# One tile fewer turned on TensorE in every second block, and key quarters loaded behind the query loads

## The chip, the cores and the metric

The kernel runs on one core of a Trainium2 chip. The metric is the device time of one execution in microseconds (us); of several executions the median counts. TensorE (PE in the profile, PEld its weight loads), VectorE (DVE), ScalarE (ACT), GpSimd (POOL) and SyncE (SP), which here only issues DMAs, each run their own stream of instructions in order and wait for each other by semaphores.

## The reference

Attention against pooled keys, and a gated MLP on the highest-scoring rows of each batch. Float32 in and out.

```
kv_pool = kv.reshape(4, 96, 4, 8, 4, 128).mean(axis=(2, 4))       # 768 keys a batch
k = v = kv_pool.reshape(4, 768, 128) @ w_sr
a = softmax(q @ k^T / sqrt(128))                                  # 12288 queries a batch
x = a @ v
per batch: take the 128 rows of x with the highest x . w_gate
           x[row] += sigmoid(score) * (relu(x[row] @ w1) @ w2)
```

## The kernel before

The queries are cut into 192 blocks of 256, 48 a batch, and one loop runs over them (`i`). A block has 256 x 768 scores, seen as 12 tiles of 128 x 128: two halves of 128 queries (`j`), six key tiles each. Every score tile is computed from split operands with three products into one of two PSUM buffers `s` (`S_together`), each of three banks of 512 columns. Then, for block `i`:

- VectorE takes the row maximum over all 1536 columns (`s_max`, tile `m`), once in every block: its starts mark the blocks in the trace.
- ScalarE takes the exponentials in three pieces (`exp`), into `am` in SBUF.
- The weights `a` are needed with the keys on the partitions, so every tile has to be turned, and each is needed twice, as a float16 high half and a bfloat16 low half. There are three ways for a tile, and `turned(n)` and `own(n)` say how many tiles go which way. **Turned on TensorE**: `turn_pe` transposes the last `turned(n)` tiles back into the `s` bank; ScalarE casts them to the high half (`to_high(n, 2)`) and VectorE subtracts for the low half (`to_low(n, 2, dve)`), both straight into `at`. **Turned by DMA**: ScalarE casts `main(n)` columns of `am` to `hl` (`to_high(n, 0)`), GpSimd makes their low halves (`to_low(n, 0, pool)`), and one DMA transpose on SP's queue (`turn`) carries both halves from `hl` to `at`. **Own**: where `own(n)` is 256, two of the tiles that go by DMA keep their exponentials in the `s` bank; ScalarE casts them from there (`to_high(n, 1)`), and VectorE rather than GpSimd makes their low halves, one block later (`to_low(i - 1, 1, dve)`, right behind `s_max(i)`).
- The product with the values (`AV`, tile `o_two`) of block `n` runs five blocks later, in two halves of 18 matmuls. Then `sums`, `recip`, `gate_scores` and `finish` on VectorE scale the rows, and every second block a store of 256 KB is issued.

In the kernel before, `turned(n)` is 2 and `own(n)` is 0 in all 144 blocks of batches 0 to 2. In batch 3, `turned(n)` is 0 in even and 1 in odd blocks, and `own(n)` is 256 in both (the last three blocks are handled apart).

Beside the blocks, tasks are advanced at marked points of the loop: `next_keys` pools and projects the keys of the next batch (GpSimd adds, seven blocks for one of six key tiles of 1 MB), `topk` searches the threshold of the batch before in 32 steps, one a block, each with a small count matmul, and `pick` runs the MLP. Batch 3 has no next keys to make.

SP's queue takes in order: in block `i` the transpose of block `i - 1`; in odd blocks the load of the queries of two blocks (256 KB, eight blocks ahead); in even blocks a store. The key tiles come in quarters of 256 KB: before, `next_keys` issues them, in steps of two blocks within a key tile, in odd blocks for one tile and in even blocks for the next, and at four even blocks at the end of a batch (`early`). The buffer `kvp` holds three key tiles.

Of the kernel before, what the change touches and what calls it, by code (L numbers as in the profile page):

```python
# [20 lines left out]
B, N, C = 4, 12288, 128  # L21
HK, WK, R = 384, 32, 4
M = (HK // R) * (WK // R)
KT = M // P
# [44 lines left out]
def attention_topk_mlp(ctx, tc, a, outs, capacity):  # L69
# [56 lines left out]
    def load_kv(b, kc, parts=1, t=None):  # L126
        late = t is not None
        if not late:
            t = kvp.tile([P, 2, P // 2, TAPS], F32, name="kv_raw")
        n = 2 // abs(parts)  # L130
        for i in range(abs(parts)):
            if parts > 0 or late == (i > 0):
                sp.dma_start(out=t[:, i * n:(i + 1) * n], in_=a["kv"][:, b, kc, i * n:(i + 1) * n])
        return t

    def load_quarter(b, kc, k, t=None):
        if t is None:
            t = kvp.tile([P, 2, P // 2, TAPS], F32, name="kv_raw")
        i, lo = k // 2, k % 2 * P // 4
        sp.dma_start(out=t[:, i, lo:lo + P // 4], in_=a["kv"][:, b, kc, i, lo:lo + P // 4])  # L140
        return t
# [3 lines left out]
    def load_q(b, ch, lo=0, hi=CHUNK):  # L145
        if (b, ch) not in qraw:
            qraw[b, ch] = qp.tile([P, CHUNK], F32, name="q_raw")
        sp.dma_start(out=qraw[b, ch][:, lo:hi], in_=a["q"][:, b, ch, lo:hi])
# [163 lines left out]

    def next_keys(b):
        new_keys(b)
        raws = {}
        pend = []
        ready = None

        def after(kc):
            if kc % 2:  # L320
                pair = kc // 2
                soon.append(lambda: (v_max(b, pair), pair == KT // 2 - 1 and v_peak(b)))
                pend.extend([lambda: None, lambda: (split_k(b, 2 * pair, 2 * pair + 2, 0), split_k(b, 2 * pair, 2 * pair + 2, 1))])

        for kc in range(KT):
            if kc == 0:
                raws[0] = early.pop(b) if b in early else load_kv(b, 0)
            if kc + 1 < KT:
                raws[kc + 1] = load_quarter(b, kc + 1, 0)
            t = raws[kc]  # L330
            pooled = kvs.tile([P, P], F32, name="pooled")
            u = kvu.tile([P, P, TAPS // 2], F32, name="kv_sum")
            t = t.rearrange("p h k t -> p (h k) t")
            adds = [(u[:, 32 * h:32 * h + 32], t[:, 32 * h:32 * h + 32, 0:8], t[:, 32 * h:32 * h + 32, 8:16]) for h in range(4)]
            adds += [(u[:, :, 0:4], u[:, :, 0:4], u[:, :, 4:8]), (u[:, :, 0:2], u[:, :, 0:2], u[:, :, 2:4]),
                     (pooled, u[:, :, 0], u[:, :, 1])]
            for h, (o, x, y) in enumerate(adds):
                if ready and h == 1:
                    yield from key_tile(b, kc - 1, ready)
                    after(kc - 1)  # L340
                yield "e" if h == len(adds) - 1 else "d"
                pool.tensor_tensor(out=o, in0=x, in1=y, op=ALU.add)
                if h == len(adds) - 1:
                    yield "d"
                if h in (1, 3, 5) and kc + 1 < KT:
                    load_quarter(b, kc + 1, (h + 1) // 2, raws[kc + 1])
                if pend:
                    pend.pop(0)()
            ready = pooled
        yield "d"  # L350
        yield from key_tile(b, KT - 1, ready)
        after(KT - 1)
        while pend:
            yield "d"
            pend.pop(0)()
        start(vals, v_split(b))
# [65 lines left out]
    def direct(n):  # L422
        return n >= nb - NDIR

    def turned(n):
        return 2 if n < 3 * NBLK else 0 if direct(n) else n % 2

    def together(n):
        return EARLY <= n < nb - NDIR - 1
# [321 lines left out]
        advance(prep, point)  # L751
        advance(select, point)

    early = {}
    now = [0]
    start(vals, first_values())
    nb = len(blocks)
    LAG, TURN, NDIR, EARLY = 5, 7, 3, 4
    spare = [s_buf[i][:, 2 * k:2 * k + 2].rearrange("p k q -> p (k q)")[:, 0:QT * VC].rearrange("p (j c) -> p j c", j=QT) for i, k in ((0, 0), (1, 1), (1, 2), (1, 0))]
    gates = s_flat[0][:, BANK:BANK + M]  # L760
# [31 lines left out]
    for i in range(nb):  # L792
        now[0] = i
        m = i - LAG + (i < TURN)
        old = m >= 0 and i != TURN
        b, blk = blocks[i]
        if i >= nb - NBLK // 2 - 4 and constants:
            pool.memset(*constants.pop(0))
        elif i >= nb - NBLK // 2 and len(spread) > 0:
            spread.pop(0)()  # L800
        if blk == 0 and b + 1 < B:
            start(prep, next_keys(b + 1))
        if b + 2 < B and blk in range(NBLK - 8, NBLK, 2):
            early[b + 2] = load_quarter(b + 2, 0, (blk - NBLK + 8) // 2, early.get(b + 2))
        if i:
            borrow(s_flat[(i - 1) % 2])
        if i == nb - 1:
            room["select"] = lot
            key = tk.tile([P, NCOL], I32, name="key")
            high = tk.tile([P, NCOL], U16, name="high")  # L810
            part = kvu.tile([P, P, TAPS // 2], F32, name="kv_sum").rearrange("p k t -> p (k t)")[:, 0:M]
            done = NCOL - QT * (LAG + 1)
            key_part(0, done)
        s_max(i)
        if i == nb - 1:
            for k in range(KT):
                pe.transpose(gates[:, k * P:(k + 1) * P], kvset[b]["raw"][:, k, 2 * P:].broadcast_to([P, P]), ident)
        if old:
            AV(m, 0)
        if i and not old:  # L820
            warm(24, banks[0][:, 0:P])
        InOrder.seen.clear()
        at_point("pe")
        side = list(InOrder.seen)
        if old:
            AV(m, 1)
        mine = []
        if i:
            if own(i - 1):
                mine = [to_low(i - 1, 1, dve)]  # L830
                for y in side:
                    tc.declare_no_dep(mine[0], y, reason="other banks")
            turn(i - 1, (0, 1) if together(i - 1) else (1,))
        if i == 0:
            split_q(*blocks[2])
        if i % 2 and i - 1 + BPC < nb:
            nb_, nblk = blocks[i - 1 + BPC]
            load_q(nb_, nblk // BPC, nblk % BPC * BLK, (nblk % BPC + 2) * BLK)
        InOrder.seen.clear()
        for point in ("ev", "up", "t", "cmp", "g"):  # L840
            at_point(point)
        side = list(InOrder.seen)
        for x in side:
            for y in mine:
                tc.declare_no_dep(x, y, reason="other banks")
        more = 0 < i < nb - 1
        groups = ((2,), (1,), (3, 0)) if room["used"] else ((3, 2), (), (1, 0))
        clear = {0: mine, 1: side, 2: side, 3: mine if room["used"] else mine + side}

        def score(k):  # L850
            if more:
                S_together(i + 1, groups[k], clear)

        score(0)
        if direct(i):
            exp(i, 3)
        else:
            exp(i, 2)
            exp(i, 1)
        if i == nb - 1:  # L860
            AV(tail[0], 0, spare[0])
        score(1)
        turn_pe(i)
        if turned(i) and i < nb - 1:
            to_high(i, 2)
        exp(i, 0)
        score(2)
        if i == nb - 1:
            AV(tail[0], 1, spare[0])
        if i == nb - 1:  # L870
            for k in range(NDIR - 1, 0, -1):
                for j in range(QT):
                    gate_sum(i - k, 1 - j)
        if old:
            sums(m)
            recip(m)
            gate_scores(m)
            if i < nb - 1:
                finish(m)
        if soon:  # L880
            soon.pop(0)()
        at_point("b")
        if turned(i):
            to_low(i, 2, dve)
        if i < nb - 1:
            if own(i):
                to_high(i, 1)
            to_high(i, 0)
            if not together(i):
                turn(i, (0,))  # L890
            to_low(i, 0, pool)
        else:
            to_high(i, 0)
            turn(i, (0,))
            to_low(i, 0, pool)
            turn(i, (1,))
            for f in late:
                f()
        if i == 0:
            warm(24, banks[0][:, 0:P])  # L900
        at_point("e")
        if i % 2 and i + 3 < nb:
            split_q(*blocks[i + 3])
        at_point("d")
        if old and blocks[m][1] == NBLK - 1:
            start(select, topk(blocks[m][0]))
# [269 lines left out]
```

## Time and profile before

| what | us |
| --- | --- |
| median of 3 executions | 915.52 |
| lowest and highest | 911.6 and 917.99 |
| the profiled execution, its own time | 911.39 |
| its span, first to last instruction | 909.6 |
| TensorE, busy in the span | 885.7 |
| GpSimd, busy in the span | 738.9 |

The span is what the rows below divide up; 1.8 us of the profiled execution's time lie around it. The profiled execution is 4.1 us below the median of the runs.

### The profile page before, as it was taken

To read this page: it belongs to the slowest core of one execution; us is meant where nothing else is said; L and a number is where in the kernel's file an instruction comes from. 1 tells how busy PE (TensorE), PEld (TensorE's weight loads), DVE (VectorE), ACT (ScalarE), POOL (GpSimd) and SP (SyncE) were. 2 spreads that over 40 slices of the span, in tenths; PEclk is the share of its full clock that TensorE was granted. 3 is DMA by queue.
4 is the path that set the end of the run, shared out by engine and by line. 5 is a ranking of instruction groups with operands and counts; after the bars stand their busy time and mean duration, and the time that the engine had idled before them with its cause. 6 is when DMAs were issued, how large, how long until landed. Compare 5 with 4: busy or idle time off the path is not lost. (4 is left out here: it accounts for less than half of the span.)

```text
span 909.6 us, 25847 instructions
## 1 busy us (share of the span) xinstructions
PE 885.7 (97%) x10179; PEld 745.9 (82%) x10179; DVE 702.3 (77%) x1855; ACT 757.1 (83%) x1240; POOL 738.9 (81%) x513
## 2 busy tenths in 40 slices
PE   5999999999999999999999999999999999999987
PEld 4788888888888888888888888888888888888865
DVE  6767767767678887887767887888776888888894
ACT  2888888888988888888988888888898888988852
POOL 2799988998899989988878898998887777777721
PEclk9999999999999999999999999999999999999999
DMA  9899999999999999999999999999999999999960
GB/s 364 193 238 234 252 227 257 241 236 231 242 230 231 224 228 247 236 240 230 250 250 236 219 241 247 247 238 230 210 215 202 251 236 251 245 251 238 236 133 22
DMA packets 557882, 209.83 MB, mean 231 GB/s; under 512 B 521408, under 2 KB 522944, under 8 KB 557376
## 3 DMA queue, kind: packets, MB, share of 16 engines
q1 hardware_dynamic: 557504, 207.66, 107.2%
q8 instruction: 79, 1.29, 0.6%
q0 software_dynamic: 256, 0.52, 0.3%
q14 instruction: 43, 0.35, 0.1%
HBM read 52.04 MB, written 25.43 MB: 85 GB/s over the span
## 5 line engine op out<-in xcount | busy, mean ns | idle before, releaser
L54 POOL TENSOR_TENSOR hl<-am,hl 128x1280 bf16<-128x1280 f32 (+2 forms) x191 | 497.3, 2604 | 115.8 <-ACT hl L54 56.9
L54 PE MATMUL o_two<-vx,at 128*128 128x130 f16 x6768 | 428.0, 219 | 0.3 <-DMA at<-hl 0.3
L54 PEld LDWEIGHTS <-at 128*128 128x128 f16 (+1 forms) x6912 | 397.9, 97 | 33.0 <-issue 31.7
L54 ACT ACTIVATE am<-s,m 128x512 f32<-128x512 f32 (+1 forms) x526 | 357.0, 706 | 34.1 <-DVE m L54 19.6
L54 DVE TENSOR_REDUCE m<-s 128x2 f32<-128x1536 f32 (+1 forms) x192 | 336.4, 1752 | 46.5 <-PE s L54 46.2
L54 PE MATMUL s<-kh,qh 128*128 128x256 f32 (+1 forms) x771 | 254.4, 407 | 0.0
L54 ACT CAST hl<-am 128x1280 f16<-128x1280 f32 (+2 forms) x191 | 239.2, 1252 | 4.7
L54 PE MATMUL s<-kl,qh 128*128 128x256 bf16 (+1 forms) x771 | 241.4, 325 | 0.0
L54 PE MATMUL s<-kb,ql 128*128 128x256 bf16 (+1 forms) x771 | 241.1, 325 | 0.1
L54 PEld LDWEIGHTS s<-kh,qh 128*128 128x128 f32 x771 | 133.0, 190 | 30.1
L54 POOL TENSOR_TENSOR ql<-q_raw,qh 128x512 bf16<-128x512 f32 x96 | 123.1, 1282 | 10.7 <-ACT qh L54 10.7
L54 DVE TENSOR_TENSOR at<-s,at 128x256 bf16<-128x256 f32 (+1 forms) x166 | 67.3, 405 | 80.2 <-ACT at L54 79.5
L54 ACT CAST at<-s 128x256 f16<-128x256 f32 (+1 forms) x166 | 59.4, 358 | 60.9 <-PE s L54 60.7
L54 PEld LDWEIGHTS <-qh 128*128 128x128 bf16 x771 | 75.1, 97 | 28.9 <-issue 3.6
L54 PEld LDWEIGHTS <-ql 128*128 128x128 bf16 x771 | 75.0, 97 | 27.5 <-POOL ql L54 0.5
L54 DVE TENSOR_TENSOR x<-o_two,rz 128x256 f32<-128x256 f32 x186 | 77.5, 417 | 0.0
L54 DVE TENSOR_SCALAR rz<-o_two,sg 128x2 f32<-128x2 f32 x187 | 40.5, 216 | 32.2 <-PE o_two L54 31.7
L54 PE MATMUL s<-cst,am 128*128 128x128 f32 x310 | 61.8, 275 | 2.2 <-ACT am L54 2.1
L54 ACT CAST qh<-q_raw 128x512 fp32r<-128x512 f32 x96 | 59.4, 619 | 3.6 <-DMA q_raw<-in_q 3.6
L54 POOL TENSOR_TENSOR kv_sum<-kv_raw 128x256 f32<-128x256 f32 x72 | 52.5, 729 | 0.0
L54 PEld LDWEIGHTS s<-cst,am 128*128 128x128 f32 x310 | 38.8, 140 | 12.8 <-ACT am L54 6.0
L54 PEld LDWEIGHTS <-ones 128*128 128x128 bf16 x353 | 29.3, 104 | 8.9 <-issue 2.7
(215 smaller groups left out, 564.6 us busy)
## 6 DMA issues: line engine op xcount, KB each, us to landing
out<-x SPq DMA_DIRECT2D x94, 256.0 KB, 2.9
q_raw<-in_q SPq DMA_DIRECT2D x93, 256.0 KB, 3.5
kv_raw<-in_kv SPq DMA_DIRECT2D x70, 256.0 KB, 3.8
at<-hl SPq DMA_TRANSPOSE x200, 5.6
kv_raw<-in_kv SPq DMA_DIRECT2D x3, 1024.0 KB, 8.9
kv_raw<-in_kv SPq DMA_DIRECT2D x5, 512.0 KB, 7.0
q_raw<-in_kv SPq DMA_DIRECT2D x2, 512.0 KB, 9.9
w<-in_w SPq DMA_DIRECT2D x2, 512.0 KB, 8.1
```

The lines of the kernel that those rows point to most:

```text
L54: r = f(*args, **kwargs)
```

## The change

In even blocks of batches 0 to 2 TensorE turns one tile rather than two. With that `own(n)` becomes 256 there, by its own rule (`turned(n) < 2`), so `main(n)` falls from 1280 to 1152 columns, and 22 half tiles go by DMA rather than 20. Odd blocks keep two tiles and no own columns. Batch 3 is as before. The key quarters are taken from one list, in order, and issued in odd blocks right behind the query load, one a block and two in blocks 9 and 11; the last goes out in block 131. The first key tile of batch 1 is still loaded whole.

```diff
-        raws = {}
...
         for kc in range(KT):
-            if kc == 0:
-                raws[0] = early.pop(b) if b in early else load_kv(b, 0)
-            if kc + 1 < KT:
-                raws[kc + 1] = load_quarter(b, kc + 1, 0)
-            t = raws[kc]
+            t = raws[b, kc] if (b, kc) in raws else load_kv(b, kc)
...
-                if h in (1, 3, 5) and kc + 1 < KT:
-                    load_quarter(b, kc + 1, (h + 1) // 2, raws[kc + 1])
...
     def turned(n):
-        return 2 if n < 3 * NBLK else 0 if direct(n) else n % 2
+        return 1 + n % 2 if n < 3 * NBLK else 0 if direct(n) else n % 2
...
-    early = {}
+    raws = {}
+    quarters = [(b, kc, k) for b in range(1, B) for kc in range(KT) for k in range(4) if (b, kc) != (1, 0)]
...
+    AHEAD = (9, 11)
...
-        if b + 2 < B and blk in range(NBLK - 8, NBLK, 2):
-            early[b + 2] = load_quarter(b + 2, 0, (blk - NBLK + 8) // 2, early.get(b + 2))
...
             load_q(nb_, nblk // BPC, nblk % BPC * BLK, (nblk % BPC + 2) * BLK)
+        for _ in range((1 + (i in AHEAD)) * (i % 2)):
+            if quarters:
+                kb_, kc, k = quarters.pop(0)
+                raws[kb_, kc] = load_quarter(kb_, kc, k, raws.get((kb_, kc)))
```

## Rows read from the trace of the kernel before

**Rows 1.** The page's first part: busy us, share of the span, instructions.

```profile
PE 885.7 (97%) x10179; PEld 745.9 (82%) x10179; DVE 702.3 (77%) x1855; ACT 757.1 (83%) x1240; POOL 738.9 (81%) x513
```

**Rows 2.** Busy time by stretch, batches 1, 2, 3: us, PE, PEld, DVE, ACT, POOL.

```profile
233.50:445.80 212.30, 211.96 (x2471) 179.93 (x2468) 168.96 (x445) 184.49 (x291) 190.02 (x129) 1.00 1.15 236
445.80:662.60 216.80, 215.87 (x2506) 183.64 (x2504) 169.41 (x449) 186.17 (x296) 192.26 (x132) 1.00 1.10 236
662.60:849.70 187.10, 187.10 (x2204) 156.63 (x2202) 153.99 (x425) 167.33 (x276) 143.22 (x98) 1.00 1.15 237
```

**Rows 3.** Timeline of DVE, batch 0, two blocks without search: start, us.

```profile
97.76 1.76 DVE L54 TENSOR_REDUCE m<-s 128x2 f32<-128x1536 f32 x1 [0.17 <-PE s L54]
...
106.35 1.76 DVE L54 TENSOR_REDUCE m<-s 128x2 f32<-128x1536 f32 x1 [0.17 <-PE s L54]
```

**Rows 4.** Timeline of DVE, batch 1, two tiles turned, search running.

```profile
281.63 1.76 DVE L54 TENSOR_REDUCE m<-s 128x2 f32<-128x1536 f32 x1 [0.17 <-PE s L54]
...
285.36 0.42 DVE L54 TENSOR_TENSOR at<-s,at 128x256 bf16<-128x256 f32 x1 [0.44 <-ACT at L54]
285.95 1.76 DVE L54 TENSOR_REDUCE m<-s 128x2 f32<-128x1536 f32 x1 [0.17 <-PE s L54]
```

**Rows 5.** Timeline, batch 3, search running: a block that turns none, then one.

```profile
708.08 1.76 DVE L54 TENSOR_REDUCE m<-s 128x2 f32<-128x1536 f32 x1 [0.39 <-PE s L54]
...
712.19 1.76 DVE L54 TENSOR_REDUCE m<-s 128x2 f32<-128x1536 f32 x1 [0.50 <-PE s L54]
...
713.87 0.41 DVE L54 TENSOR_TENSOR hl<-s,hl 128x256 bf16<-128x256 f32 x1
...
714.52 0.27 PE L54 MATMUL s<-kl,qh 128*128 128x256 bf16 x1
...
716.40 1.76 DVE L54 TENSOR_REDUCE m<-s 128x2 f32<-128x1536 f32 x1 [0.39 <-PE s L54]
```

**Rows 6.** Timeline of PE, batch 1: two transposes and the matmul behind them.

```profile
284.54 0.38 PE L54 MATMUL s<-cst,am 128*128 128x128 f32 x2
284.75 0.27 PE L54 MATMUL s<-kl,qh 128*128 128x256 bf16 x1
```

**Rows 7.** Groups by shape, count | busy us, mean ns | idle before, releaser.

```profile
L54 POOL TENSOR_TENSOR hl<-am,hl 128x1280 bf16<-128x1280 f32 x167 | 438.7, 2627 | 76.7 <-ACT hl L54 43.6 <-PE s L54 13.9 <-POOL kv_sum L54 4.8
L54 PE MATMUL o_two<-vx,at 128*128 128x130 f16 x6768 | 428.0, 219 | 0.3 <-DMA at<-hl 0.3
...
L54 PE MATMUL s<-cst,am 128*128 128x128 f32 x310 | 61.8, 275 | 2.2 <-ACT am L54 2.1
...
L54 POOL TENSOR_TENSOR hl<-am,hl 128x1152 bf16<-128x1152 f32 x22 | 52.5, 2384 | 36.5 <-PE s L54 18.9 <-ACT hl L54 10.7 <-issue 7.0
...
L54 ACT CAST hl<-s 128x256 f16<-128x256 f32 x45 | 16.6, 368 | 0.0
```

**Rows 8.** Timeline of SP's queue, end of batch 2, behind queries alone.

```profile
648.41 2.58 SPq L54 DMA_TRANSPOSE at<-hl  x1
```

**Rows 9.** Timeline of SP's queue, batch 3: the first and last of eight transposes.

```profile
763.32 3.12 SPq L54 DMA_TRANSPOSE at<-hl  x1
...
792.64 3.24 SPq L54 DMA_TRANSPOSE at<-hl  x1
```

**Rows 10.** Timeline of SP's queue, batch 1: 29 transposes from first to last row.

```profile
270.50 3.73 SPq L54 DMA_TRANSPOSE at<-hl  x1
...
341.02 2.84 SPq L54 DMA_TRANSPOSE at<-hl  x1
...
392.62 0.42 SPq L54 DMA_DIRECT2D kv_raw<-in_kv  x1
393.15 3.89 SPq L54 DMA_TRANSPOSE at<-hl  x1
...
397.77 2.71 SPq L54 DMA_TRANSPOSE at<-hl  x1
```

**Rows 11.** Timeline of POOL, batch 1: the low halves that the transpose at 341.02 carries.

```profile
331.26 2.62 POOL L54 TENSOR_TENSOR hl<-am,hl 128x1280 bf16<-128x1280 f32 x1 [1.25 <-PE s L54]
```

## The prediction

> **What bounds the kernel now.** I read the busy shares first. TensorE is busy for 97% of the span, the others for 77 to 83% [rows 1]; a busy TensorE is not yet a full one, since its matmuls overlap. So the second view is a clock of the blocks: the start of the row maximum on VectorE, once a block, and the difference of two starts is what a block costs. With two tiles turned and no search running it is 4.295 us (8.59 for two blocks) [rows 3]; with the search, 4.32 [rows 4]; in batch 3, with the search, 4.11 for a block that turns none and 4.21 for one that turns one [rows 5]. The pitch follows the number of transposes on TensorE, although batch 3 differs in much else: less GpSimd work (143 of 187 us against 190 of 212), more ScalarE work (167 of 187 against 184 of 212) [rows 2]. What the other engines do less or more leaves no mark. That is how a bound engine looks: TensorE sets the block, in every batch. VectorE waits 0.17 us for TensorE's scores ahead of each maximum [rows 3, 4], not the reverse.
>
> The third view is SP's queue, because the change gives it more. Its rows stand almost without a gap in batch 1: 29 transposes from 270.50 to 397.77 are 28 steps in 127.27 us, 9.09 us for a pair of blocks [rows 10], where the batch as a whole runs at 212.3/24 = 8.85 us a pair [rows 2]. The queue was falling behind: low halves that GpSimd finished at 331.26 + 2.62 = 333.88 [rows 11] were sent off at 341.02 [rows 10], 7.1 us later. No one paid for it: the values' matmuls waited 0.3 us for turned tiles in the whole run [rows 7], as they come five blocks later. The second resource, right under TensorE, is thus the DMA queue.
>
> **The change, part by part.**
>
> *One transpose less on TensorE* in 72 even blocks (24 in each of three batches). Three rows price it. Two transposes take 0.21 us up to the next matmul's start, 0.105 each [rows 6]; from two to one is 4.32 - 4.21 = 0.11 with the search running [rows 4, 5]; from one to none 0.10 [rows 5]. I take 0.11 for all: 72 x 0.11 = 7.9 us, all on the path that sets the end; with 0.10 it is 7.2, with 0.12 8.6. Recorded durations are another matter: the mean transpose has 275 ns [rows 7], but the matmul behind it starts before it ends.
>
> The Trainium skill (TensorE: Matmul & The Clock Gate, Part 4) also says about 275 ns for a transpose in one kernel's context. By that figure the saving would be an estimated 72 x 0.275 = 19.8 us; the pitch of the blocks here speaks for 0.11.
>
> *VectorE* gets the own columns' low halves: 0.41 us per even block [rows 5], queued behind the next block's maximum; its subtraction of turned tiles, 0.42 [rows 4], has half the columns then and shrinks by 0 to 0.2. Behind it on VectorE stand the search step and the scaling of rows in the odd block. In the block before it had 0.44 us idle ahead of the turned tiles' low halves and 0.17 ahead of the maximum [rows 4], so 0.61 us covers 0.41: zero on the path. TensorE waits for the same instruction: the scores of the block after reuse its bank. In batch 3 it ends at 713.87 + 0.41 = 714.28, and the first matmul into that bank starts at 714.52 [rows 5]: 0.24 us to spare. In blocks where the pick uses PSUM, that bank's matmuls come first, and the spare is gone: about 12 such odd blocks in batches 1 and 2, at zero to 0.24 us. I charge 0.4 us, with 0 and 2.9 as ends.
>
> *ScalarE* casts the same 1536 columns in three pieces rather than two; one piece more costs at most the whole 0.368 us of the own cast [rows 7]. Its share in batch 1 is 87%, and with 24 x 0.37 = 8.9 us more it would be 91%, next to batch 3's 89% [rows 2] with all blocks at TensorE's pitch. Zero. *GpSimd* loses 2.627 - 2.384 = 0.24 us per even block [rows 7]: it had 90% in batch 1 [rows 2]; it gains room, no time.
>
> *SP's queue, transposes.* 22 half tiles in an even block's transpose for 20: per pair two more. With no key loads about, a transpose of 20 takes 2.58 [rows 8], 0.13 a half tile, so +0.26 us a pair.
>
> *SP's queue, key quarters.* Before, about eight in seven pairs while a batch's tiles are loaded; now one a pair. A quarter takes 0.42 to issue, and the transpose behind it is slower: 3.89 [rows 10] against 2.58 [rows 8], up to 1.3 more. What moves past what: in odd blocks the quarter now stands ahead of the next block's transpose, and the load is never late, since by the loop's steps a quarter is issued 3 to 11 blocks before GpSimd reads it. Nor does it wait for a buffer: with three, the one that it takes was last read at least ten blocks earlier. So the whole price is queue time. For a pair after the change I have two bounds. From batch 3: two transposes of 23 half tiles on average, at a mean 3.34 over eight [rows 9], and two copies at the 0.42 of one of the same size [rows 10], make 7.5; less four half tiles (0.5), plus a quarter with its drag (0.4 to 1.7): 7.4 to 8.7. From batch 1: 9.09 + 0.26, less a seventh of a quarter with its drag (0.25): 9.1. TensorE would give 8.85 - 0.11 = 8.74 a pair. I take 8.6, inside the range of batch 3, which holds the nearest number of tiles, but at its upper end towards batch 1; the queue then stays just below TensorE.
>
> **Sum.** -7.9 + 0.4 = -7.5 us. Against the profiled execution 911.39 - 7.5 = 903.9; the median of the runs is 4.1 above it, so 915.5 - 7.5 = 908.0, or 0.8% less.
>
> **Rivals.**
>
> *The transposes' queue becomes the bound* (slower). It is issued in order, and it has the two extra half tiles per pair with no fewer copies. For it: the 7.1 us lag in batch 1 [rows 10, 11]. Against it: batch 3 carries more tiles without falling behind (seven steps in 792.64 - 763.32 = 29.32 us are 4.19 a block, TensorE's own pitch) [rows 9]. At 9.1 a pair against 8.74, in the 62 pairs from block 8 to 131, it falls behind by 62 x 0.36 = 22 us. About 6 us of lag are free (7.1 cost nothing), and the slow blocks of the pick between batches 1 and 2 give about 6 back. So TensorE waits 10 us for turned tiles: 908.0 + 10 = 918. It decides from 8.74 + (12 + 7.5)/62 = 9.05 a pair on; at 9.2 it would be 924, slower by 1%.
>
> *More comes back than the transposes.* Batch 2 has the same work as batch 1 and took 216.8 against 212.3 us [rows 2]. If those 4.5 us are waits for a late GpSimd or a crowded queue, which the lighter GpSimd and the even key loads end, it is -12: 903.5.
>
> *TensorE is not full.* What the rows show is a pitch that follows the transposes [rows 3 to 5]. If it followed something else that batch 3 has less of, the key work, nothing would change: 915.5.
>
> The Trainium skill (Perfetto Trace Analysis, Identifying the Most-Contended Engine) says that matmul busy time misleads and that the weight loads' busy share tells TensorE's headroom. That share is 82% [rows 1], so by the rule the engine has room and this rival would hold. The step of 0.10 us within batch 3 itself, with neither key work nor a change of buffers between the two blocks, speaks against it.
>
> *A transpose is worth its recorded 275 ns* [rows 7]: 915.5 - 19.8 = 895.7. The 0.21 us for two [rows 6] speaks against it.
>
> **How the numbers follow.** A difference under 1% (9.2 us) is about what a measurement here can tell from none. Forecast, 905 to 911: 0.55, of which 0.11 lies below 906.4. Queue as bound, 912 to 926: 0.18, of which 0.08 is over 1% slower. More comes back, 900 to 906: 0.17, nearly all over 1% faster (0.16). TensorE not full: 0.07. 275 ns: 0.03. Faster 0.11 + 0.16 + 0.03 = 0.30; slower 0.08; the rest 0.62. The range 901 to 918 leaves out the end of the second case, most of the 275 ns case and a little of the third.
>
> **What would show it.** Right: 4.21 us for even blocks with the search and 4.18 without, odd ones as before, 238 transposes on TensorE for 310, the own subtraction 72 times more on VectorE with no new wait of TensorE behind it, and no more than 0.3 us of waits for turned tiles. Wrong: values' matmuls that wait for DMA, a lag between GpSimd's low halves and their transpose that grows past 7 us over a batch, or odd blocks that lengthen.

## The result and the profile after

The changed kernel takes 920.12 us (median of 17 runs, 912.84 to 926.95), the kernel before 912.32 in the same session (17 runs, 910.51 to 917.99). The ratio is 1.0064, with a 95% interval of 1.0042 to 1.0085: slower by 0.6%, where 0.8% less was forecast, and outside the range of 901 to 918. Ratio and interval, here and below, leave out executions in a slower state (here the one of 926.95), and are not the ratio of the two medians, which is 1.0085. The profiled execution took 920.73 us, its span is 918.9, against 909.6 before.

The page's first part, as in [rows 1]:

```profile
PE 881.5 (96%) x10107; PEld 738.2 (80%) x10107; DVE 716.9 (78%) x1927; ACT 759.3 (83%) x1312; POOL 721.8 (79%) x513
```

TensorE has 72 instructions less and VectorE 72 more, so the change did what it says. But TensorE's share fell, in a span that grew: it has work taken away and stands idle longer. Busy time by stretch, batches 1 and 2 of the changed kernel, columns as in [rows 2]:

```profile
237.30:456.00 218.70, 210.75 (x2447) 177.54 (x2448) 174.41 (x469) 185.18 (x315) 184.45 (x129) 1.00 1.14 241
456.00:671.80 215.80, 213.93 (x2482) 180.96 (x2480) 173.97 (x474) 186.91 (x320) 186.39 (x132) 1.00 1.16 243
```

Batch 1 took 212.3 us and takes 218.7; TensorE, busy in all but 0.3 us of it [rows 2], has 8 us of idle time. Batch 2 gained 1.0 us. Batch 0, from its first row maximum to that of batch 1, took 209.4 us (24.03 to 233.47) and takes 212.6 (24.68 to 237.28). What TensorE waits for is in the groups by shape of the changed kernel (columns as in [rows 7]):

```profile
L54 POOL TENSOR_TENSOR hl<-am,hl 128x1280 bf16<-128x1280 f32 x95 | 249.3, 2625 | 89.6 <-ACT hl L54 63.8 <-PE s L54 11.9 <-POOL kv_sum L54 3.6
L54 PE MATMUL o_two<-vx,at 128*128 128x130 f16 x6768 | 427.8, 219 | 13.5 <-DMA at<-hl 12.9 <-DVE x L54 0.3
...
L54 PE MATMUL s<-cst,am 128*128 128x128 f32 x238 | 53.8, 275 | 1.0 <-ACT am L54 0.8
...
L54 DVE TENSOR_TENSOR hl<-s,hl 128x256 bf16<-128x256 f32 x117 | 48.5, 415 | 0.0
```

The transposes are 238 for 310, as forecast. The values' matmuls, which waited 0.3 us in the whole run [rows 7], wait 12.9 us for turned tiles (`at<-hl` is the transpose by DMA). The waits of the changed kernel, as us in total, times, longest, show that the weight loads ahead of those matmuls wait too, and ScalarE behind them, for the buffer that the transpose still reads:

```profile
PEld L54 <- DMA at<-hl: 22.5, 33, 2.0
...
PE o_two L54 <- DMA at<-hl: 12.9, 21, 1.7
...
ACT hl L54 <- DMA at<-hl: 9.1, 16, 1.5
...
PE s L54 <- DVE hl L54: 1.1, 2, 0.8
```

These lines overlap (a late tile stops a weight load and its matmul), so they are not added up. The last one is TensorE waiting for VectorE's own subtraction. The clock of the blocks, starts of the row maximum on VectorE in batch 0 of the changed kernel:

```profile
76.13 1.76 DVE L54 TENSOR_REDUCE m<-s 128x2 f32<-128x1536 f32 x1 [0.17 <-PE s L54]
80.32 1.76 DVE L54 TENSOR_REDUCE m<-s 128x2 f32<-128x1536 f32 x1 [0.41 <-PE s L54]
84.61 1.76 DVE L54 TENSOR_REDUCE m<-s 128x2 f32<-128x1536 f32 x1 [0.17 <-PE s L54]
...
106.26 1.76 DVE L54 TENSOR_REDUCE m<-s 128x2 f32<-128x1536 f32 x1 [0.41 <-PE s L54]
110.55 1.76 DVE L54 TENSOR_REDUCE m<-s 128x2 f32<-128x1536 f32 x1 [0.17 <-PE s L54]
116.02 1.76 DVE L54 TENSOR_REDUCE m<-s 128x2 f32<-128x1536 f32 x1 [0.41 <-PE s L54]
```

An undisturbed block with one transpose takes 4.19 us (forecast 4.18), one with two 4.29, as before [rows 3]. The block from 110.55 on is again one of the short kind, and takes 5.47: 1.28 too long. PE's timeline in that block gives the reason in its brackets:

```profile
111.62 2.24 PE L54 MATMUL o_two<-vx,at 128*128 128x130 f16 x36 [1.11 <-DMA at<-hl]
```

SP's queue in the changed kernel around this wait, and two lines for the pace: the transposes that start at 100.19 and at 438.82 are 75 steps apart.

```profile
71.30 0.91 SPq L54 DMA_DIRECT2D kv_raw<-in_kv  x2
72.31 5.83 SPq L54 DMA_TRANSPOSE at<-hl  x1
...
100.19 2.84 SPq L54 DMA_TRANSPOSE at<-hl  x1
103.08 0.57 SPq L54 DMA_DIRECT2D q_raw<-in_q  x1
103.69 0.43 SPq L54 DMA_DIRECT2D kv_raw<-in_kv  x1
104.24 3.88 SPq L54 DMA_TRANSPOSE at<-hl  x1
108.21 0.52 SPq L54 DMA_DIRECT2D out<-x  x1
108.90 3.78 SPq L54 DMA_TRANSPOSE at<-hl  x1
...
438.82 3.75 SPq L54 DMA_TRANSPOSE at<-hl  x1
```

Between the rows there is nothing but 0.04 to 0.17 us: the queue is full. A pair takes (438.82 - 100.19)/75 x 2 = 9.03 us. The third line is late: GpSimd's timeline of the changed kernel has the low halves that it carries done at 90.36 + 2.37 = 92.73,

```profile
90.36 2.37 POOL L54 TENSOR_TENSOR hl<-am,hl 128x1152 bf16<-128x1152 f32 x1
```

and they are sent 7.46 us later. This lag (end of the low halves to the start of their transpose) was 0.5 us at block 9 and 7.5 at block 14, which is this one; it stays between 4.7 and 9.9 through the rest of batches 0 and 1, between 3 and 7.4 in batch 2 up to the last key quarter, and at 3.0 or less in batch 3. In the kernel before it was 0 to 3 in batch 0 and rose to 7.1 in batch 1 alone [rows 10, 11].

So the profile shows the first two signs of "wrong" that the prediction listed, the waits and the lag. What remains to be shown is which part of the change does it (more tiles by DMA, the place of the key loads, the double loads in blocks 9 and 11), what in the queue is scarce, and whether the forecast saving exists at all.

### The profile page after: what moved, and what is told of

Read it like the earlier page. It is cut to its first block, busy times and chain, and to the rows that moved or that the text cites. A ratio compares the mean times of both kernels' runs of the same rounds, so it can differ in the third digit from the quotient of the medians.

```text
span 918.9 us, 25853 instructions
## 1 busy us (share of the span) xinstructions
PE 881.5 (96%) x10107; PEld 738.2 (80%) x10107; DVE 716.9 (78%) x1927; ACT 759.3 (83%) x1312; POOL 721.8 (79%) x513
## 5 line engine op out<-in xcount | busy, mean ns | idle before, releaser
L54 POOL TENSOR_TENSOR hl<-am,hl 128x1280 bf16<-128x1280 f32 (+2 forms) x191 | 479.6, 2511 | 141.8 <-ACT hl L54 87.0
L54 PE MATMUL o_two<-vx,at 128*128 128x130 f16 x6768 | 427.8, 219 | 13.5 <-DMA at<-hl 12.9
L54 ACT ACTIVATE am<-s,m 128x512 f32<-128x512 f32 (+2 forms) x454 | 330.9, 746 | 37.1 <-DVE m L54 28.3
L54 ACT CAST hl<-am 128x1280 f16<-128x1280 f32 (+2 forms) x191 | 233.0, 1220 | 10.2 <-DMA at<-hl 8.1
L54 DVE TENSOR_TENSOR at<-s,at 128x128 bf16<-128x128 f32 (+1 forms) x166 | 57.7, 348 | 57.2 <-ACT at L54 54.7
L54 ACT CAST at<-s 128x128 f16<-128x128 f32 (+1 forms) x166 | 51.7, 312 | 55.0 <-PE s L54 52.6
L54 ACT ACTIVATE s<-s,m 128x256 f32<-128x256 f32 x117 | 52.4, 448 | 3.8
L54 PE MATMUL s<-cst,am 128*128 128x128 f32 x238 | 53.8, 275 | 1.0 <-ACT am L54 0.8
L54 DVE TENSOR_TENSOR hl<-s,hl 128x256 bf16<-128x256 f32 x117 | 48.5, 415 | 0.0
```

The lines of the kernel that those rows point to most:

```text
L54: r = f(*args, **kwargs)
```

## The experiments

Times are medians; the ratio is to runs of the kernel before on the same chip, whose medians were 913.40 (the first four), 913.12 (the next four) and 913.34 (the last three). The waits are of the one profiled execution, which for e8_half and e11_skip_loads was the longest of its runs.

| run | us | lowest to highest | ratio, 95% interval | values' matmuls wait for DMA, us |
|---|---|---|---|---|
| e1_tiles | 924.33 | 921.30 to 928.59 | 1.0128, 1.0093 to 1.0162 | 17.4 |
| e2_loads | 914.54 | 910.78 to 918.69 | 1.0011, 0.9988 to 1.0034 | 1.9 |
| e3_ahead | 920.54 | 919.09 to 921.95 | 1.0081, 1.0052 to 1.0110 | 12.2 |
| e4_actq | 924.04 | 919.21 to 925.19 | 1.0103, 1.0063 to 1.0144 | 14.9 |
| e5_light_after | 903.95 | 903.60 to 904.16 | 0.9878, 0.9850 to 0.9907 | 0 |
| e6_light_before | 911.31 | 910.71 to 911.63 | 0.9965, 0.9947 to 0.9984 | 0 |
| e7_where_idle | 912.90 | 908.29 to 916.16 | 0.9982, 0.9957 to 1.0007 | 2.9 |
| e8_half | 921.35 | 916.49 to 924.64 | 1.0073, 1.0048 to 1.0097 | 12.9 |
| e9_late | 910.11 | 909.24 to 913.65 | 0.9964, 0.9944 to 0.9984 | 3.7 |
| e10_skip | 910.42 | 905.30 to 914.91 | 0.9961, 0.9938 to 0.9984 | 7.1 |
| e11_skip_loads | 911.56 | 907.50 to 920.48 | 0.9973, 0.9956 to 0.9989 | 13.2 |

**The tiles alone.** The kernel before, with the new rule for the turned tiles and the old key loads:

```diff
-        return 2 if n < 3 * NBLK else 0 if direct(n) else n % 2
+        return 1 + n % 2 if n < 3 * NBLK else 0 if direct(n) else n % 2
```

> The changed turning alone: one tile on TensorE in even blocks, own columns on VectorE, key quarters issued where they were before. Theory A (the two more half tiles a pair overload the in-order transposes' queue by themselves): the lag between GpSimd's low halves and their transpose passes 6 us in batches 0 to 2, values' matmuls wait for DMA, 916 to 921 us. Theory B (the key quarters behind the queries, and the doubled ones in blocks 9 and 11, do it; the tiles alone fit): lag mostly under 4 us, 904 to 907 us. Rival C (VectorE's own subtraction holds TensorE up in odd blocks): 916 to 921 us without waits for DMA.

924.3 us, 4 us above the whole change and above what was expected of any theory, with a lag of 5 to 9.6 us from block 14 to the end of batch 1 and of 3.4 to 8.4 in batch 2 up to block 131. The new rule for the turned tiles does the harm by itself; the new place of the loads takes some of it away. The rule makes TensorE faster and gives the queue more tiles at once; e10_skip below separates the two.

**The loads alone.** The changed kernel with two transposes in every block of batches 0 to 2:

```diff
-        return 1 + n % 2 if n < 3 * NBLK else 0 if direct(n) else n % 2
+        return 2 if n < 3 * NBLK else 0 if direct(n) else n % 2
```

> The changed key loads alone: two tiles turned on TensorE in all blocks of batches 0 to 2, as before. Theory A: no loss, 911 to 914 us, lag under 7 us as before. Theory B: the queue falls behind from block 9 on and stays behind, 916 to 922 us. Rival C: as before, 911 to 914 us.

914.5, not to be told from the kernel before. The lag is 4 to 6 us in batch 0 from block 20 on and 7.8 at most, at the end of batch 1, and the values' matmuls wait 1.9 us in all. While the tiles stay on TensorE the move of the loads costs no time that shows, though it fills the queue's slack earlier: the lag of the kernel before was 0 to 3 in batch 0.

**The double loads elsewhere.** In blocks 9 and 11 the change issues two quarters, and the transpose behind them takes 5.83 us (at 72.31 above) and 5.21. Here they stand in blocks 5 and 7:

```diff
-    AHEAD = (9, 11)
+    AHEAD = (5, 7)
```

> The changed kernel with the doubled quarters in blocks 5 and 7 rather than 9 and 11, where the queue still waits for GpSimd. If the two doubled loads use up the free lag and the rest of the run only keeps it (theory B in part): the lag at block 14 is under 4 us rather than 7.5, and the time falls to 913 to 916 us. If each pair asks too much of the queue (theory A): the lag gets to 7 us some 10 pairs later, 918 to 920 us. Rival C: no change, 920 us.

920.5, as the change. The lag rises later (3.9 us at block 15, 7.0 at block 24) and then stays at 5 to 9 through batch 1. The doubles fill the slack early; without them the steady excess fills it some ten blocks later. It is the pace that costs, not the two blocks.

**The key loads off SP's queue.** The changed kernel, quarters issued by ScalarE:

```diff
-        sp.dma_start(out=t[:, i, lo:lo + P // 4], in_=a["kv"][:, b, kc, i, lo:lo + P // 4])
+        act.dma_start(out=t[:, i, lo:lo + P // 4], in_=a["kv"][:, b, kc, i, lo:lo + P // 4])
```

> The changed kernel with the key quarters issued on ScalarE's queue: the same bytes on the same DMA engines, but the transposes don't queue behind the issue of a quarter in SP's stream. If SP's order of issue is the limit: transposes behind queries alone take 2.9 to 3.1 us rather than 3.8, the lag stays under 3 us, 903 to 907 us. If the DMA engines' time is the limit: the transposes lengthen wherever the quarters run, 916 to 921 us. Rival C: no change, 920 us.

924.0: no better. SP's queue in this run:

```profile
275.68 0.57 SPq L54 DMA_DIRECT2D q_raw<-in_q  x1
276.35 2.86 SPq L54 DMA_TRANSPOSE at<-hl  x1
279.31 0.52 SPq L54 DMA_DIRECT2D out<-x  x1
280.00 4.31 SPq L54 DMA_TRANSPOSE at<-hl  x1
```

and a quarter among ScalarE's issues, by the same timeline:

```profile
278.92 0.33 ACTq L54 DMA_DIRECT2D kv_raw<-in_kv  x1
```

The quarter no longer takes SP's 0.43 us, but the transpose that starts 1.1 us after it takes 4.31 where the one ahead took 2.86. A store stands ahead of the long one, a query load ahead of the short one, and so it is on the whole: in batches 0 and 1, 4.3 to 4.5 us in the mean behind stores, 3.3 behind query loads. In the changed kernel, where the quarter goes out behind the query load, it is the reverse, 3.1 to 3.2 behind stores and 3.9 to 4.0 behind query and key loads. The long transpose goes where the quarter goes, whichever engine issues it. The quarter's issue had ended at 279.25, 0.75 us before the long transpose began, so it is not the issue that lengthens it. What is scarce is thus not SP's order of issue; the rows point to the work behind the issue, which the quarter's bytes and the transposes share.

**Three of four quarters left out.** The same edit on the changed kernel (e5_light_after) and on the kernel before (e6_light_before):

```diff
+        if k:
+            return t
...
-            adds = [(u[:, 32 * h:32 * h + 32], t[:, 32 * h:32 * h + 32, 0:8], t[:, 32 * h:32 * h + 32, 8:16]) for h in range(4)]
+            adds = [(u[:, 32 * h:32 * h + 32], t[:, 0:32, 0:8], t[:, 0:32, 8:16]) for h in range(4)]
```

> The changed kernel with three of four key quarters not loaded (GpSimd pools the first quarter of a tile four times, so the keys of batches 1 to 3 are not the reference's; every instruction but the loads is kept). Theory A (TensorE's saving is there, the load on the transposes' DMAs hides it): the lag stays under 4 us, no waits for turned tiles, even blocks 4.19 to 4.22 us throughout, 903 to 906 us. Against theory A (the new order of work on VectorE, ScalarE or TensorE costs the time): 915 us or more.

> The kernel before with the same three of four key quarters not loaded. If TensorE bounds the kernel before and its queue only runs close behind: 911 to 913 us, no gain, and a lag under 2 us in batch 1 too. If the queue already costs the kernel before something: 906 to 909 us.

The two runs belong together: with room in the queue the change is worth 911.31 - 903.95 = 7.36 us, where 7.5 was forecast. In batches 0 to 2 the lag is at most 1.6 us in either, and in neither do the values' matmuls wait for DMA; the row of e5_light_after, by shape:

```profile
L54 PE MATMUL o_two<-vx,at 128*128 128x130 f16 x6768 | 427.8, 219 | 0.3 <-DVE x L54 0.3
```

Its blocks in batch 1 (VectorE's timeline, search running) take 4.32 and 4.22 us, the 4.32 and 4.21 of the prediction:

```profile
270.83 1.76 DVE L54 TENSOR_REDUCE m<-s 128x2 f32<-128x1536 f32 x1 [0.41 <-PE s L54]
275.15 1.76 DVE L54 TENSOR_REDUCE m<-s 128x2 f32<-128x1536 f32 x1 [0.17 <-PE s L54]
279.37 1.76 DVE L54 TENSOR_REDUCE m<-s 128x2 f32<-128x1536 f32 x1 [0.41 <-PE s L54]
```

And its transposes from 102.29 to 436.25 on SP's queue, 77 steps, go at TensorE's pace, (436.25 - 102.29)/77 x 2 = 8.67 us a pair, with 3.07 us each in the mean against 3.49 in the changed kernel (78 and 76 rows of the stretch 100 to 440):

```profile
102.29 2.92 SPq L54 DMA_TRANSPOSE at<-hl  x1
...
436.25 2.62 SPq L54 DMA_TRANSPOSE at<-hl  x1
```

TensorE's new wait for VectorE's own subtraction is there too:

```profile
PE s L54 <- DVE hl L54: 2.1, 3, 1.4
```

The changed kernel loses 920.12 - 903.95 = 16.2 us to the queue. The kernel before loses some 1 to 2 (912.3 to 913.1 against 911.31).

**The change where the queue had seemed idle.** Old loads, one transpose in even blocks of 4 to 12 and 98 to 108, and one or none in blocks 132 to 143:

```diff
-        return 2 if n < 3 * NBLK else 0 if direct(n) else n % 2
+        if 4 <= n <= 12 or 98 <= n <= 108:
+            return 1 + n % 2
+        return 2 if n < 132 else 0 if direct(n) else n % 2
```

> The kernel before with fewer tiles turned on TensorE only where its queue shows no lag: one tile in even blocks from 4 to 12 and 98 to 108, and none in even, one in odd blocks from 132 to 143, after the last key load. 11 + 18 transposes fewer at 0.11 are 3.2 us. Theory A: 908 to 910 us against the kernel before's 912 to 913, with a lag that goes back under 3 us outside these blocks. If every further half tile by DMA costs time wherever it is: 912 us or more.

912.9, no difference. Five more tiles in blocks 4 to 12 leave a lag of 3 to 7 us through the rest of batch 0, where the kernel before has 0 to 3: what is put into the queue there is not worked off before batch 1 wants the slack. The waits for turned tiles on the weight loads are 5.1 us.

**Half the tiles.** The changed kernel with one transpose in every fourth block:

```diff
-        return 1 + n % 2 if n < 3 * NBLK else 0 if direct(n) else n % 2
+        return 1 + (n % 4 > 0) if n < 3 * NBLK else 0 if direct(n) else n % 2
```

> Half of the change: one tile on TensorE in every fourth block of batches 0 to 2, two in the others, with the changed key loads. TensorE alone would give 912.5 - 4 = 908.5 us. Theory A with the queue's demand just over TensorE's pitch at the full change: demand falls by 0.13 us a pair and TensorE's pitch is 0.05 longer, so some 11 us of the full change's 15 us of waits go: 909 to 913 us. If the queue is over its limit with the key loads alone: 914 to 917 us.

921.4, as much as the whole change; 909 to 913 was expected, or 914 to 917 if the loads alone were too much. With half the tiles TensorE has half the saving, and the waits are nearly those of the whole change. This was not explained: see below.

**A transpose left out, and nothing in its place.** The kernel before without one of the two transposes of even blocks in batches 0 to 2; no tile goes to DMA in its stead:

```diff
+            if c == 0 and n % 2 == 0 and n < 3 * NBLK:
+                continue
```

> The kernel before, with the first of the two transposes on TensorE left out in even blocks of batches 0 to 2 and nothing put in its place (ScalarE casts the scores that lie there, so those tiles of the output are not the reference's). TensorE's pitch is the changed kernel's, the DMAs' work is the kernel before's. Theory A (the two more half tiles a pair are what the queue can't take): 904 to 907 us, lag under 7 us, hardly a wait. Theory D (the queue of the kernel before already runs at its own limit, some 8.8 to 8.9 us a pair, and any time that TensorE saves is waited away): 910 to 914 us, with values' matmuls that wait for DMA, although not one tile more is turned by it.

910.4: 2.9 us of some 7.4 come back. Its groups by shape show the tiles by DMA unchanged (167 pieces of 1280 columns, as in [rows 7]), the transposes 238 as after the change, and TensorE waiting for turned tiles all the same:

```profile
L54 POOL TENSOR_TENSOR hl<-am,hl 128x1280 bf16<-128x1280 f32 x167 | 438.6, 2626 | 77.7 <-ACT hl L54 48.6 <-PE s L54 12.7 <-POOL kv_sum L54 4.3
...
L54 PE MATMUL o_two<-vx,at 128*128 128x130 f16 x6768 | 428.1, 219 | 7.2 <-DMA at<-hl 7.1
...
L54 PE MATMUL s<-cst,am 128*128 128x128 f32 x238 | 53.9, 276 | 2.1 <-ACT am L54 1.8
```

The queue of the kernel before had no room under a faster TensorE, even with no tile more. If a transpose is worth here what it is in e5_light_after, some 4.5 us are waited away at once. The tiles that go over to the queue cost the rest: with the old loads 924.3 - 910.4 = 13.9 us (e1_tiles against this run), with the new ones 920.1 - 911.6 = 8.5 (the change against the next run).

The same with the new place of the key loads (the changed kernel, with these lines):

```diff
-        return 1 + n % 2 if n < 3 * NBLK else 0 if direct(n) else n % 2
+        return 2 if n < 3 * NBLK else 0 if direct(n) else n % 2
...
+            if c == 0 and n % 2 == 0 and n < 3 * NBLK:
+                continue
```

> The same left-out transpose, with the changed key loads. Theory A: 904 to 908 us. Theory D: 910 to 915 us. If the new place of the key quarters helps once TensorE is faster, it is below the run with the old loads by 2 us or more.

911.6, against 910.4: the new place of the loads buys the queue nothing here. The 13.2 us of waits in the table are of the profiled execution, at 920.48 the longest of its runs; the median run cannot have had as many.

**The change late in batch 2 alone.** In the kernel before the lag is some 2 us in batch 2, and the last key quarter goes out at 606 us, about block 132; behind it the queue has room to work a lag off. So the tiles move from block 98 on alone: one of an even block's up to 131, then both of an even block's and one of an odd one's up to 143, 35 in all. Old loads:

```diff
-        return 2 if n < 3 * NBLK else 0 if direct(n) else n % 2
+        if 98 <= n < 132:
+            return 1 + n % 2
+        return 2 if n < 132 else 0 if direct(n) else n % 2
```

> The kernel before with fewer tiles turned on TensorE late only: one in even blocks from 98 to 131, where the slow blocks of the pick have just emptied the queue, then none in even and one in odd blocks from 132 to 143, after the last key load. 17 + 18 transposes fewer at 0.11 are 3.9 us. Theories A and D alike: the lag grows from about 1 us at block 100 by at most 0.4 us a pair and doesn't reach 7 us before the last key load, so nearly all of it comes back: 908 to 910 us beside 912 to 913 for the kernel before. If waits start wherever a tile is added: 912 us or more.

910.1, 3.2 us less than the kernel before (0.9964, 0.9944 to 0.9984), 10 less than the changed one. The lag is 1.5 us at block 100, 3.3 at block 103 and 8.4 at block 124, more than the 7 that was expected not to be reached: even this little fills the slack before the loads end. Nor is the lag worked off behind them, where yet more tiles go over; it is 4 to 6 us in blocks 132 to 143 and 3.3 to 7.5 in batch 3, where the kernel before has at most 2.1. The waits of this run on the weight loads:

```profile
PEld L54 <- DMA at<-hl: 9.3, 17, 1.4
```

Of the kernels that compute the whole, this is the fastest; the margin is small, but the interval lies below 1. It does not tell this kernel from e7_where_idle.

## Why the prediction was wrong

**TensorE's saving was right.** 72 transposes at 0.11 us less 0.4 for VectorE made 7.5 us; with room in the queue the runs give 7.36, and the blocks have the pitches that were forecast. So TensorE was full, and the rival that it is not is out. The Trainium skill (Perfetto Trace Analysis, Identifying the Most-Contended Engine) has TensorE's headroom judged by the weight loads' busy share, or by its share of peak arithmetic. By the first, 82% [rows 1], there was room here; the runs show none. A transpose is worth 7.36/72 = 0.10 us, not the 0.275 that its rows show.

**VectorE, ScalarE and GpSimd** cost little, as charged. VectorE's 72 more subtractions did make TensorE wait, 1.1 us in the changed kernel and 2.1 in e5_light_after, against 0.4 charged with 0 to 2.9 as ends; the 7.36 has that in it.

**The key quarter's price was inside its range.** Two transposes a pair at 3.49 rather than 3.07 are 0.84 us, and 0.75 of an issue of 0.43 is 0.32: 1.16 us for three quarters of a load, so about 1.5 for one; the prediction had 0.4 to 1.7.

**The step that failed is "I take 8.6"** for the queue's work in a pair, "the queue then stays just below TensorE". The pair takes 9.03; TensorE offers 8.67 (8.74 was forecast). The rows allow the sum again: two transposes 6.98, the query load 0.57, the quarter 0.43, the store 0.52, and five gaps between rows of 0.47 in all (from 100.19 to 108.90 above) make 8.97. The prediction's lower bound, from batch 3, took 0.42 for each of the copies where they take 0.57 and 0.52, and left out the gaps, which were there to be read in the queue of before. Its 7.4 to 8.7 should have been 8.1 to 9.4, and with 1.5 for the quarter 9.2, next to the 9.1 of the other bound, from batch 1. That bound was right, and the prediction put it aside for the one with "the nearest number of tiles".

**Behind it is a misreading of the lag.** The 7.1 us in batch 1 [rows 10, 11] were read as harmless, since the waits of the whole run were 0.3 us. They were slack being used up: the kernel before ran into the queue's limit in batch 1 and was let out at its end, where no quarter goes out between blocks 84 and 89 and then the slow blocks of the pick come (its lag is 6.1 us at block 82, 4.0 at 88 and 0 at 100). e10_skip shows the limit, where a faster TensorE waits at once. A queue that falls behind a pace of 8.85 us a pair cannot keep up with 8.74.

**So the first rival came**, with its place and its cause: forecast 918 with 10 us of waits, measured 920.1 with 16.2. Its excess was right, 9.1 - 8.74 = 0.36 us a pair against 9.03 - 8.67 = 0.36. It counted some 12 us of lag as free or given back; if 62 x 0.36 = 22 is the whole, about 6 was. Against e5_light_after the profiled execution loses 5.4 us in batch 0, 9.7 in batch 1 and 2.0 in batch 2. That 918 came so near is in part luck: it started from 915.5, the median of three, where 17 runs have 912.3, and that made up for about half of the missing waits.

**The second rival** (more comes back, 903.5) did not: batch 2 gained 1.0 us, where 24 transposes are worth 2.6. Nor were the 4.5 us between batches 1 and 2 waits for a crowded queue: in e5_light_after, without those waits, batch 2 takes 213.7 and batch 1 209.1 us.

**What stays open.** Where the queue is backed up in batch 1 its work in a pair measures 9.0 to 9.1 us whether 40 half tiles (kernel before, 9.09 [rows 10]), 41 (e8_half) or 42 (the change) go through it, so the sum by tiles, 0.13 us a half tile, does not describe it. That is why e8_half was expected too fast; what sets the pace in that state was not found. That the limit lies behind SP's issue is shown as far as e4_actq and e5_light_after go: the loads cost the queue with and without SP's issue, and without most of them it has room. That it is the time of the 16 DMA engines is argued, not shown. Their mean busy share, the last column but one of the stretches, does not tell: it is 1.14 in batch 1 of the changed kernel and 1.15 in batch 3 of the kernel before [rows 2], where the lag is at most 2.1 us.

## What to carry to other kernels

Before crediting a saving on the bound engine, work out the pitch of the second resource from its own rows, gaps included, and compare it with the pitch that the first will have; here 9.03 us a pair against 8.67 took back twice what was saved. A lag that grows between a producer and its DMA is slack being spent, and zero waits say only that it isn't spent yet. Where a tile can go to either of two nearly full resources, where it is moved counts as much as how many are: 36 tiles spread evenly cost 8 us (e8_half, with the new loads), 35 from block 98 on, shortly before the loads end, gained 3 (e9_late, with the old).

## What the runs showed of the hardware

The row of a DMA transpose of 20 half tiles on SP's queue takes 2.58 us behind queries alone [rows 8], 3.88 (at 104.24) behind a query load and a key quarter of 256 KB each, and 5.83 (at 72.31) behind a query load and two quarters. Issuing the quarter on ScalarE's queue does not take the lengthening away: it moves to the transpose that follows the quarter in time (2.86 and 4.31 in e4_actq).

The spread of the kernel before, 910.5 to 918.0 us over 17 runs, shrinks to 910.7 to 911.6 over 12 runs when three of four key quarters are left out, and that of the changed kernel from 912.8 to 927.0 to 903.6 to 904.2 (6 runs). So most of this variation comes with the crowded DMA queue: the instructions of the five engines are the same with and without the quarters.
